# Two heads side by side in the array's rows, for the token products of a chunked attention

## Chip, cores and metric

One core of a Trainium2 chip runs one program. The metric is device time in microseconds (us), the median of the runs shown. Engines are named as the profile names them: PE (TensorE, its weight loads are PEld), DVE (VectorE), ACT (ScalarE), POOL (GpSimd), SP (SyncE, which here issues the DMAs).

## Reference

A linear attention with a state per head (4 batches, 8 heads, 768 tokens, 40 channels) is followed by a mixture of experts and a second feed-forward layer. Only the attention is touched here:

```python
for t in range(S):
    y[:, :, t] = np.einsum('bhd,bhde->bhe', rt, state)
    Sa = np.einsum('bhde,bhe->bhd', state, at)
    state_decay = state * wt[:, :, None, :] - np.einsum('bhd,bhe->bhde', Sa, bt)
    state = state_decay + np.einsum('bhd,bhe->bhde', vt, kt)
...
x = _moe_ref(x=x, **moe_kwargs)
return _moe2_ref(x=x, **moe2_kwargs)
```

## The kernel before

The program has two stages, one behind the other: the attention (`with ExitStack() as st`, L239 to L796), then the two feed-forward parts (L862 on), whose first matmul comes after the last instruction of the attention.

**Units.** The attention cuts the tokens into NJ = 6 chunks of C = 128. A unit n is one chunk of one batch, all 8 heads: 24 units, j = n // 4 the chunk, b = n % 4 the batch. Channels lie in the partitions, two heads in one tile: head a = 0 in rows 0 to 39, head a = 1 in rows 64 to 103 (HR = 104 rows in all), and four such pairs (HP = 4) one after the other in the free dimension. The inputs `em` come laid out so, with zeros in rows 40 to 63.

**What a unit does**, each a generator that yields segments (`Seg`):
- `decays` (L291): clamps the decays, two scans (L307, L313) for running products and their inverses, then `bt` (L326) and `at` (L329) as elementwise products, and two ACT passes that look for rare values.
- `lab_grams` (L336): the token products of `at` with `bt` (L352), evicted by ACT into `ld` (L359, four 32-row pieces a half) and `lab` (L360).
- `invert` (L373): the inverse of the small triangular blocks, on DVE and POOL, once for each chunk.
- `pre` (L421): `kt` (L432), the transposes `tp` (L438), the token products of `at` with `kt` (`lak`), the products with the old state (L458), a transpose of it (L467), and `z` (L474).
- `chain` (L479): four blocks of 32 tokens one after the other; PE (L498, L506, tiles of 32 by 32) and ACT (L502, L510) wait for each other in turn.
- `post` (L513): transposes of `u` (L522) and their copy `ut` (L525), the token products `mrv` (of `r` with `v`) and `mru` (of `r` with `u`), the state update (L539 to L547), and `yps` (L555, L566), evicted by DVE (L572).

**The token products** are made by `gram` (L405) for `lak`, `mrv` and `mru` and by `lab_grams` for `lab`: four sets in each unit. One head's channels stand in 40 of the 104 rows, and both heads of a pair are in the moving tile, so the stationary tile is padded: `bt`, `kt`, `ut`, `vt` have the shape [104, 4, 2, 128], where half a holds the rows of head a and zeros in all other rows. A matmul then goes over 104 rows, of which 64 at most are not zero by construction:

```python
for q in range(HP):
    nc.tensor.matmul(
        ps[:, q, :], lhsT=lhs[:, q, a, :], rhs=rhs[:, q, :],
        start=(q == 0), stop=True, skip_group_check=True,
    )
```

Half a = 0 makes four matmuls into one PSUM bank (`psg`, 3 buffers), is evicted (DVE L416, or ACT), then half a = 1 the same. A float32 matmul stands in the trace as two LDWEIGHTS and two MATMUL records, so a set of 8 matmuls has 16 of each. The padded tiles cost two elementwise operations each, one a half, of which the second may go to POOL (`spare_pool`, L626), and the zeros are written once by POOL (L730, L738).

**What sets the order.** The order of all instructions is written when the program is built. `drive` (L664) takes segments from nine flows by a model of the engines' clocks (`clk`): a segment has a PE time `pe`, an activity weight `w` for a model of TensorE's clock, the engine that evicts and its time, and what it needs. Where the model sees PE wait or its clock about to fall, `idle` (L651) puts in spare matmuls (L654). Each engine then runs its own list in that order.

**Start.** SP loads `e` for units 0 to 3 and 4 (L261), with nothing to wait for; `load_mid` brings `kr`, `v`, `bk`.

Of the kernel before, what the change touches and what calls it, by code (L numbers as in the profile page):

```python
# [18 lines left out]
C = 128  # L19
# [3 lines left out]
HALF = (slice(0, 64), slice(64, HR))  # L23
# [18 lines left out]
POOLED = 1  # L42
# [29 lines left out]
def tile_kernel(ctx, tc, em, tm, qr, qk, qv, qw, qa, qb, w_gate, w1, w2, u1, u2, u3, u_out, out):  # L72
# [8 lines left out]
    make_identity(nc, ident)  # L81
# [157 lines left out]
    with ExitStack() as st:  # L239
# [19 lines left out]
        def load_e(n, t):  # L259
            for c in (slice(0, WC), slice(WC, EC)) if not n else (slice(0, EC),):  # L260
                nc.sync.dma_start(out=t[:, c], in_=em[n // NB, n % NB, :, c])  # L261

        def load_late(n):
            d = un[n]
            d["rt"] = r_ring[n % 2]
            nc.sync.dma_start(
                out=d["rt"].rearrange("p g c -> p (g c)"), in_=em[n // NB, n % NB, :, EC + HP * C:EC + 2 * HP * C]
            )
            d["late"] = sent(0.6)

        def load_v(n):
            j, b = jb(n)
            for a in range(2):
                nc.sync.dma_start(
                    out=pads[3][64 * a:64 * a + D, :, a],
                    in_=em[j, b, 64 * a:64 * a + D, EC + 2 * HP * C:].rearrange("e (g c) -> e g c", c=C),
                )
            un[n]["vt_"] = sent(0.7)

        def load_mid(n):  # L280
            j, b = jb(n)
            d = un[n]
            nc.sync.dma_start(out=kr.rearrange("p g c -> p (g c)"), in_=em[j, b, :, EC:EC + HP * C])
# [7 lines left out]
        def decays(n, e, ready, bt):  # L291
# [6 lines left out]
            p = d["p"] = hold.tile([HR, HP, C + 1], F32, tag="p", name="p", bufs=LOOK + 2)  # L298
            ip = hold.tile([HR, HP, C + 1], F32, tag="ip", name="ip", bufs=LOOK)
            at = hold.tile([HR, HP, C], F32, tag="at", name="at", bufs=LOOK)  # L300
# [17 lines left out]
            d["bt_"] = []  # L318
# [14 lines left out]
            nc.scalar.activation(out=off, in_=ew, func=AF.Abs, bias=wmid)  # L333
            nc.scalar.activation(out=off, in_=off, func=AF.Relu, bias=wrad, accum_out=beyond[:, n:n + 1])

        def lab_grams(n):  # L336
# [6 lines left out]
            lab = None  # L343
            for a in range(2):
                s = Seg(pe=0.87, w=0.81, eng="A", cost=1.05, needs=[d["at_"], *d["bt_"]],
                        gate=lambda: count["chain"] > n - LOOK)
                yield s
                if lab is None:
                    lab = d["lab"] = hold.tile([C, H, C - 32], F32, tag="lab", name="lab", bufs=LOOK)
                ps = psg.tile([C, HP, C], F32, tag="g", name="psg")  # L350
                for q in range(HP):
                    nc.tensor.matmul(  # L352
                        ps[:, q, :], lhsT=bt[:, q, a, :], rhs=at[:, q, :],
                        start=(q == 0), stop=True, skip_group_check=True,
                    )
# [49 lines left out]
        def gram(lhs, rhs, res, tag, bufs, needs):  # L405
            for a in range(2):
                s = Seg(pe=0.87, w=0.81, eng="V", cost=0.6, needs=needs)
                yield s
                ps = psg.tile([C, HP, C], F32, tag="g", name="psg")
                for q in range(HP):  # L410
                    nc.tensor.matmul(  # L411
                        ps[:, q, :], lhsT=lhs[:, q, a, :], rhs=rhs[:, q, :],
                        start=(q == 0), stop=True, skip_group_check=True,
                    )
# [6 lines left out]
        def pre(n):  # L421
# [5 lines left out]
            kt_ = []  # L427
            for a, r in enumerate(HALF):
                key, eng = ("P", nc.gpsimd) if a and spare_pool() else ("V", nc.vector)
                kt_.append(Seg(eng=key, cost=1.3 if key == "P" else 0.6, needs=[d["mid"], d["ip_"]]))  # L430
                yield kt_[a]
                eng.tensor_tensor(out=kt[r, :, a], in0=kr[r], in1=ip[r], op=ALU.mult)  # L432
# [4 lines left out]
            for q in range(HP):  # L437
                nc.tensor.transpose(tp[:, q, 0:HR], ip[:, q, :], ident[0:HR, 0:HR])  # L438
# [18 lines left out]
            for q in range(HP if j else 0):  # L457
                nc.tensor.matmul(  # L458
                    zf[:, q, 0:HR], lhsT=at[:, q, :], rhs=s[:, q, :],
# [53 lines left out]
        def post(n):  # L513
            j, b = jb(n)
            d, u, s = un[n], u_ring[n % 2], s_t[b]
            ut_ = Seg(pe=0.44, eng="A", cost=1.0, needs=lambda: [d["u_"]], gate=lambda: count["chain"] > n)
# [7 lines left out]
            for a, r in enumerate((slice(0, 64), slice(64, HR))):  # L524
                nc.scalar.activation(out=ut[r, :, a], in_=ups[r], func=AF.Copy)  # L525
# [28 lines left out]
            for q in range(HP if j else 0):  # L554
                nc.tensor.matmul(  # L555
                    yps[:, q, :], lhsT=d["sd"][:, q, :], rhs=rt[:, q, :],
# [68 lines left out]

        def spare_pool():  # L626
            return clk["P"] + POOLED < max(clk["E"], clk["V"])

# [545 lines left out]
```

## Time and profile before

| | us |
|---|---|
| median of 3 runs | 2256.01 |
| the runs | 2254.65, 2272.37, 2256.01 |
| the profiled execution | 2262.95 |
| its span, first to last instruction | 2261.2 |
| PE busy in the span (share) | 2210.5 (98%) |
| DVE, ACT, POOL busy | 1108.2, 619.7, 324.2 |

All rows below are of the profiled execution, with time from the start of its span. A busy PE in such a table is the union of its records, which overlap; the distance from one run of records to the next tells what a run costs. The granted clock (PEclk) is 1.00 where TensorE ran at its level of 2.4 GHz and 0.50 at that of 1.2 GHz.

### The profile page before, as it was taken

Reading aid. Unit: us, or ns where it says so; the run is one execution under the profiler, and the core shown is the slowest. Engines: PE = TensorE matmul, PEld = TensorE weight load, DVE = VectorE, ACT = ScalarE, POOL = GpSimd, SP = SyncE. Lnnn points to the kernel's source line nnn. Section 1 sums busy time; section 2 is a strip of 40 time slices with the busy share of each in tenths; the row PEclk is TensorE's granted clock in tenths of the full one; section 3 lists DMA queues with packets and bytes.
Section 4 is the critical chain, followed back from the end, with each engine's and each line's share of the span. In section 5 each row is a group of like instructions: output and inputs, shape, how many; then the busy total and the mean of one; then the engine's idle time right before and its main releaser. Section 6 shows DMA issues by size and latency. Waiting matters only on the chain.

```text
span 2261.2 us, 37488 instructions
## 1 busy us (share of the span) xinstructions
PE 2210.5 (98%) x15933; PEld 1989.1 (88%) x15933; DVE 1108.2 (49%) x1896; ACT 619.7 (27%) x1239; POOL 324.2 (14%) x478
## 2 busy tenths in 40 slices
PE   5899999999999999999999999999999999999999
PEld 5888888899789999999989989999999999988888
DVE  8788667542344366556555443333343343442332
ACT  3544444322332133122122122121121121222221
POOL 6457356250000010011101000000000000000000
PEclk7899999997999999999999999999999999999999
DMA  4243333221201011111111000000000000100000
GB/s 114 71 123 96 102 83 88 66 82 36 66 27 33 1 39 44 43 36 56 36 39 44 25 26 20 8 26 14 13 26 12 15 27 7 55 6 21 15 12 24
DMA packets 71320, 94.98 MB, mean 42 GB/s; under 512 B 6981, under 2 KB 55877, under 8 KB 71149
## 3 DMA queue, kind: packets, MB, share of 16 engines
q1 hardware_dynamic: 71149, 92.56, 14.7%
q8 instruction: 125, 2.05, 0.4%
q14 instruction: 46, 0.38, 0.1%
HBM read 80.74 MB, written 11.80 MB: 41 GB/s over the span
## 4 chain that ended last, share of the span: by engine, by line
PE 74%; ACT 0%; issue 0%
PE ps L222 33%; PE ps L215 31%; PE pu L215 9%; PE gps L215 0%; PE xt L1025 0%; PE tps L909 0%; PE ct L947 0%; ACT acc L1059 0%; PE t L925 0%; PE t L919 0%
## 5 line engine op out<-in xcount | busy, mean ns | idle before, releaser
L222 PE MATMUL ps<-w2h,h 128*128 128x320 f32 x3072 | 693.0, 309 | 0.0
L222 PEld LDWEIGHTS ps<-w2h,h 128*128 128x128 f32 x3072 | 517.6, 188 | 4.5
L963 ACT ACTIVATE h<-ps 128x512 fp32r<-128x512 f32 x384 | 229.9, 599 | 999.5 <-PE ps L215 985.4
L964 DVE SCALAR_TENSOR_TENSOR h<-ps,h 128x512 fp32r<-128x512 f32 x384 | 265.7, 692 | 456.4 <-ACT h L963 455.4
L222 PE MATMUL ps<-w2l,h 128*128 128x320 f32 x1536 | 474.2, 309 | 0.0
L215 PE MATMUL ps<-xh,w1l 128*128 128x512 f32 x1152 | 330.9, 395 | 5.2 <-DVEq L856 5.2
L215 PE MATMUL ps<-xh,w1h 128*128 128x512 f32 x1152 | 327.4, 392 | 0.0
L984 DVE SCALAR_TENSOR_TENSOR acc<-ps,lg,acc 128x320 f32<-128x320 f32 x336 | 184.9, 550 | 255.2 <-PE ps L222 253.7
L222 PEld LDWEIGHTS ps<-w2l,h 128*128 128x128 f32 x1536 | 288.2, 188 | 4.0
L215 PEld LDWEIGHTS ps<-xh,w1h 128*128 128x128 f32 x1152 | 216.7, 188 | 48.6
L215 PEld LDWEIGHTS ps<-xh,w1l 128*128 128x128 f32 x1152 | 212.1, 188 | 46.5 <-issue 5.4
L215 PE MATMUL ps<-xl,w1h 128*128 128x512 f32 x768 | 239.4, 393 | 0.0
L215 PEld LDWEIGHTS ps<-xl,w1h 128*128 128x128 f32 x768 | 144.5, 188 | 34.1
L215 PE MATMUL pu<-xh,uq 128*128 128x512 f32 x648 | 171.2, 394 | 0.0
L416 DVE TENSOR_TENSOR gr<-psg,mask 128x512 f32<-128x512 f32 x144 | 97.7, 689 | 94.8 <-PE psg L411 93.8
L215 PEld LDWEIGHTS pu<-xh,uq 128*128 128x128 f32 x648 | 120.3, 188 | 25.2
L135 POOL TENSOR_TENSOR f<-f,m 128x384 f32<-128x384 f32 (+2 forms) x24 | 24.2, 1009 | 666.3 <-DVE m L133 405.7
L391 POOL TENSOR_TENSOR tmp<-lt,tt 128x87 f32<-128x87 f32 (+24 forms) x186 | 106.5, 572 | 60.3 <-DVE lt L369 46.2
L395 POOL TENSOR_TENSOR tt<-tt,tmp 128x87 f32<-128x87 f32 (+24 forms) x186 | 110.6, 595 | 14.6
L1045 DVE TENSOR_TENSOR g<-pu,g 128x512 f32<-128x512 f32 x72 | 49.8, 692 | 99.9 <-PE pu L215 99.9
L352 PE MATMUL psg<-at,bt 104*128 104x128 f32 x384 | 54.5, 300 | 29.8 <-DVE at L329 28.8
L510 ACT ACTIVATE u<-z 32x320 f32<-32x320 f32 x96 | 41.1, 429 | 138.0 <-PE z L506 137.9
(158 smaller groups left out, 2359.4 us busy)
## 6 DMA issues: line engine op xcount, KB each, us to landing
e<-in_em_dram SPq DMA_DIRECT2D x23, 626.0 KB
r<-in_moe_w_dram SPq DMA_DIRECT2D x32, 320.0 KB
r<-in_moe_w_dram SPq DMA_DIRECT2D x32, 256.0 KB
bk<-in_tm_dram SPq DMA_DIRECT2D x24, 320.0 KB
kr<-in_em_dram SPq DMA_DIRECT2D x24, 208.0 KB
r<-in_em_dram SPq DMA_DIRECT2D x24, 208.0 KB
raw<-in_moe_w_dram SPq DMA_DIRECT2D x12, 384.0 KB
r<-in_moe_w_dram SPq DMA_DIRECT2D x64, 64.0 KB
```

The costliest lines, as they stand in the source:

```text
L135: nc.gpsimd.tensor_tensor(out=f, in0=f, in1=m.bitcast(F32), op=ALU.mult)
L215: nc.tensor.matmul(ps, lhsT=a, rhs=b, start=(n == 0), stop=(n == len(seq) - 1))
L222: nc.tensor.matmul(ps, lhsT=a, rhs=b, start=(n == 0), stop=(n == last))
L352: nc.tensor.matmul(ps[:, q, :], lhsT=bt[:, q, a, :], rhs=at[:, q, :], start=(q == 0), stop=True, skip_group_check=True,)
L391: eng.tensor_tensor(out=t, in0=lt[:, m:m + 1, m + 1:32].to_broadcast([128, n, w]), in1=tt[:, 0:n, m:m + 1].to_broadcast([128, n, w]), op=A ...
L395: eng.tensor_tensor(out=tt[:, 0:n, m + 1:32], in0=tt[:, 0:n, m + 1:32], in1=t, op=ALU.subtract)
L416: nc.vector.tensor_tensor(out=t, in0=ps, in1=mask.unsqueeze(1).to_broadcast([C, HP, C]), op=ALU.mult)
L510: nc.scalar.activation(out=u[r, :, 0:D], in_=zh[r, :, 0:D], func=AF.Copy)
L963: nc.scalar.activation(out=h[:, 0], in_=ps, func=AF.Relu)
L964: nc.vector.scalar_tensor_tensor(out=h[:, 1], in0=ps, scalar=0.0, in1=h[:, 0].bitcast(F32), op0=ALU.max, op1=ALU.subtract)
L984: nc.vector.scalar_tensor_tensor(out=acc[:, i], in0=ps, scalar=pr[:, i, e:e + 1], in1=acc[:, i], op0=ALU.mult, op1=ALU.add,)
L1045: nc.vector.tensor_tensor(out=g, in0=ps, in1=g, op=ALU.max)
```

## The change

The two heads of a pair get 64 rows of the array each. `bt`, `kt`, `ut`, `vt`, and `at`, `ip`, `p`, `kr`, `rt`, `e` become tiles of 128 rows, in which rows 40 to 63 and 104 to 127 are zero (or, for the decays, without effect); the padded halves are gone. A new function `products` makes both heads' matmuls in turn, head a on array rows 64a to 64a + 63, each head into a PSUM bank of its own, and both banks are evicted after it. Its segment has pe = GRAM = 1.05 where there were two of 0.87. `psg` has 4 buffers for 3, `psy` 1 for 2. `bt` and `kt` are one DVE operation each, `ut` one ACT copy, `vt` one DMA; POOL has none of them. The zeros are written into rows 96 to 127 before the first loads, and the identity is made after them.

```diff
-POOLED = 1
+GRAM = 1.05
...
-    make_identity(nc, ident)
...
-        psg = pool(st, "psg", 3, space=PSUM)
+        psg = pool(st, "psg", 4, space=PSUM)
-        psy = pool(st, "psy", 2, space=PSUM)
+        psy = pool(st, "psy", 1, space=PSUM)
...
-            for a in range(2):
-                nc.sync.dma_start(
-                    out=pads[3][64 * a:64 * a + D, :, a],
-                    in_=em[j, b, 64 * a:64 * a + D, EC + 2 * HP * C:].rearrange("e (g c) -> e g c", c=C),
-                )
-            un[n]["vt_"] = sent(0.7)
+            nc.sync.dma_start(out=pads[3][0:HR].rearrange("p g c -> p (g c)"), in_=em[j, b, :, EC + 2 * HP * C:])
+            un[n]["vt_"] = sent(0.6)
...
-            for a, r in enumerate(HALF):
-                key, eng = ("P", nc.gpsimd) if a and (n < NB or spare_pool()) else ("V", nc.vector)
-                s = Seg(eng=key, cost=1.3 if key == "P" else 0.6, needs=[d["ip_"]])
-                d["bt_"].append(s)
-                yield s
-                eng.tensor_tensor(out=bt[r, :, a], in0=eb[r], in1=d["ip"][r], op=ALU.mult)
+            d["bt_"] = Seg(eng="V", cost=0.6, needs=[d["ip_"]])
+            yield d["bt_"]
+            nc.vector.tensor_tensor(out=bt, in0=eb, in1=d["ip"], op=ALU.mult)
...
+        def products(lhs, rhs):
+
+
+            ps = [psg.tile([C, HP, C], F32, tag="g", name="psg") for _ in range(2)]
+            for q in range(HP):
+                for a in range(2):
+                    r = slice(64 * a, 64 * a + 64)
+                    nc.tensor.matmul(
+                        ps[a][:, q, :], lhsT=lhs[r, q, :], rhs=rhs[r, q, :],
+                        start=(q == 0), stop=True, skip_group_check=True, tile_position=(64 * a, 0),
+                    )
+            return ps
...
-            for a in range(2):
-                s = Seg(pe=0.87, w=0.81, eng="A", cost=1.05, needs=[d["at_"], *d["bt_"]],
-                        gate=lambda: count["chain"] > n - LOOK)
-                yield s
...
+            s = Seg(pe=GRAM, w=0.8, eng="A", cost=2.1, needs=[d["at_"], d["bt_"]],
+                    gate=lambda: count["chain"] > n - LOOK)
+            yield s
+            lab = d["lab"] = hold.tile([C, H, C - 32], F32, tag="lab", name="lab", bufs=LOOK)
+            for a, ps in enumerate(products(bt, at)):
...
-            for a in range(2):
-                s = Seg(pe=0.87, w=0.81, eng="V", cost=0.6, needs=needs)
-                yield s
...
+            s = Seg(pe=GRAM, w=0.8, eng="V", cost=1.2, needs=needs)
+            yield s
+            for ps in products(lhs, rhs):
...
-            for a, r in enumerate((slice(0, 64), slice(64, HR))):
-                nc.scalar.activation(out=ut[r, :, a], in_=ups[r], func=AF.Copy)
+            nc.scalar.activation(out=ut[0:HR], in_=ups, func=AF.Copy)
...
-            pads = [ring.tile([HR, HP, 2, C], F32, name=x) for x in ("bt", "kt", "ut", "vt")]
+            pads = [ring.tile([128, HP, C], F32, name=x) for x in ("bt", "kt", "ut", "vt")]
...
+            low = slice(96, 128)
+            nc.vector.memset(es[0][low], 0.0)
+            for t in es[1:] + [e]:
+                nc.gpsimd.memset(t[low], 0.0)
             ready = {}
+            nc.gpsimd.memset(kr[low], 0.0)
+            make_identity(nc, ident)
...
-            for t in bts + pads[1:2]:
-                nc.gpsimd.memset(t, 0.0)
...
-                for t in u_ring + s_t + pads[2:]:
+                for t in u_ring + s_t:
                     nc.gpsimd.memset(t, 0.0)
+                for t in r_ring + pads[2:]:
+                    nc.gpsimd.memset(t[low], 0.0)
```

## Rows read from the trace of the kernel before

**Rows 1.** Windows: length; busy PE, PEld, DVE, ACT, POOL; granted clock; DMA share, GB/s.

```profile
155.70:418.00 262.30, 255.19 (x3433) 234.04 (x3433) 187.22 (x283) 118.30 (x296) 140.48 (x201) 1.00 0.36 95
...
495.30:585.30 90.00, 84.73 (x1000) 77.13 (x998) 28.34 (x45) 20.00 (x43) 2.83 (x2) 0.85 0.15 41
585.30:2261.20 1675.90, 1672.57 (x9139) 1493.97 (x9139) 733.31 (x1298) 386.55 (x659) 49.09 (x48) 1.00 0.09 27
0.00:74.60 74.60, 44.25 (x285) 42.94 (x286) 65.18 (x120) 29.96 (x83) 45.45 (x93) 0.75 0.39 96
74.60:155.70 81.10, 77.13 (x1024) 70.16 (x1022) 61.00 (x95) 41.46 (x106) 47.49 (x68) 1.00 0.39 103
```

**Rows 2.** Groups by line, 155.7 to 418.0: busy us, mean ns, idle before.

```profile
L416 DVE TENSOR_TENSOR gr<-psg,mask 128x512 f32<-128x512 f32 x74 | 50.0, 687 | 28.3 <-PE psg L411 27.6
L502 ACT ACTIVATE zs<-z 32x320 f32<-32x320 f32 x48 | 20.4, 424 | 43.4 <-PE z L498 43.3
L326 DVE TENSOR_TENSOR bt<-e,ip 64x512 f32<-64x512 f32 (+1 forms) x22 | 18.4, 838 | 0.3
L432 DVE TENSOR_TENSOR kt<-kr,ip 64x512 f32<-64x512 f32 (+1 forms) x18 | 16.8, 933 | 0.7
L329 DVE TENSOR_TENSOR at<-e,p 104x512 f32<-104x512 f32 x13 | 11.3, 867 | 0.1
```

**Rows 3.** Timeline of PE, 190 to 200: start us, us, what, records, idle before.

```profile
191.95 1.90 PE L474 MATMUL z<-v,gr 128*128 128x40 f32 x16
193.67 0.62 PE L522 MATMUL ups<-ident,u 128*104 128x128 f32 x4
194.13 1.95 PE L352 MATMUL psg<-at,bt 104*128 104x128 f32 x16
195.92 1.06 PE L411 MATMUL psg<-r,vt 104*128 104x128 f32 x8
197.22 1.16 PE L411 MATMUL psg<-r,vt 104*128 104x128 f32 x8 [0.24 <-ACT lab L360]
198.71 0.27 PE L539 MATMUL dps<-v,kb 128*40 128x40 f32 x2 [0.33 <-ACT lab L360]
```

**Rows 4.** Timeline of PE, 203 to 212.

```profile
204.36 0.76 PE L506 MATMUL z<-zs,td 32*32 32x40 f32 x16
205.04 1.07 PE L566 MATMUL yps<-gr,kb 128*40 128x128 f32 x16
206.05 0.76 PE L498 MATMUL z<-u,lab 64*32 64x40 f32 x16
```

**Rows 5.** Groups by line, 0 to 74.6: the `lab` products.

```profile
L352 PE MATMUL psg<-at,bt 104*128 104x128 f32 x96 | 18.4, 371 | 29.2 <-DVE at L329 28.8 <-ACT off L333 0.4
```

**Rows 6.** Timeline of ACT, 190 to 200: the eviction of `lab`.

```profile
195.55 1.11 ACT L359 ACTIVATE ld<-psg 32x128 f32<-32x128 f32 x4
...
198.55 0.41 ACT L502 ACTIVATE zs<-z 32x320 f32<-32x320 f32 x1
```

**Rows 7.** Timeline of all engines, 0 to 16: the start.

```profile
0.80 2.11 SPq L261 DMA_DIRECT2D e<-in_em_dram  x5
1.15 0.49 DVE L726 MEMSET ends<- 104x517 f32 x1
3.92 2.16 DVE L306 TENSOR_SCALAR e<-e 104x512 f32<-104x512 f32 x1 [2.01 <-DMA e<-in_em_dram]
9.57 0.68 DVE L329 TENSOR_TENSOR at<-e,p 104x512 f32<-104x512 f32 x1
14.40 1.70 POOL L326 TENSOR_TENSOR bt<-e,ip 40x512 f32<-40x512 f32 x1 [3.11 <-DVE ip L313]
14.96 1.68 DVE L329 TENSOR_TENSOR at<-e,p 104x512 f32<-104x512 f32 x1
```

**Rows 8.** Windows late in the attention.

```profile
510.00:530.00 20.00, 20.00 (x153) 18.07 (x154) 2.77 (x4) 4.61 (x10) 0.00 (x0) 0.53 0.04 10
550.00:560.00 10.00, 10.00 (x138) 9.29 (x135) 2.96 (x5) 2.24 (x5) 0.00 (x0) 1.00 0.15 39
```

More of the change, by code (lines that the diff above doesn't have):

```diff
@@ L22 @@
 HR = 64 + D
-HALF = (slice(0, 64), slice(64, HR))
 WC = HP * (C + 1) + 1
@@ L260, in load_e @@
             for c in (slice(0, WC), slice(WC, EC)) if not n else (slice(0, EC),):
-                nc.sync.dma_start(out=t[:, c], in_=em[n // NB, n % NB, :, c])
+                nc.sync.dma_start(out=t[0:HR, c], in_=em[n // NB, n % NB, :, c])
         def load_late(n):
@@ L266, in load_late @@
             nc.sync.dma_start(
-                out=d["rt"].rearrange("p g c -> p (g c)"), in_=em[n // NB, n % NB, :, EC + HP * C:EC + 2 * HP * C]
+                out=d["rt"][0:HR].rearrange("p g c -> p (g c)"), in_=em[n // NB, n % NB, :, EC + HP * C:EC + 2 * HP * C]
             )
@@ L282, in load_mid @@
             d = un[n]
-            nc.sync.dma_start(out=kr.rearrange("p g c -> p (g c)"), in_=em[j, b, :, EC:EC + HP * C])
+            nc.sync.dma_start(out=kr[0:HR].rearrange("p g c -> p (g c)"), in_=em[j, b, :, EC:EC + HP * C])
             d["v"] = tokp.tile([C, H, D], F32, tag="v", name="v", bufs=3)
@@ L297, in decays @@
             yield d["ip_"]
-            p = d["p"] = hold.tile([HR, HP, C + 1], F32, tag="p", name="p", bufs=LOOK + 2)
-            ip = hold.tile([HR, HP, C + 1], F32, tag="ip", name="ip", bufs=LOOK)
-            at = hold.tile([HR, HP, C], F32, tag="at", name="at", bufs=LOOK)
+            p = d["p"] = hold.tile([128, HP, C + 1], F32, tag="p", name="p", bufs=LOOK + 2)
+            ip = hold.tile([128, HP, C + 1], F32, tag="ip", name="ip", bufs=LOOK)
+            at = hold.tile([128, HP, C], F32, tag="at", name="at", bufs=LOOK)
             d["bt"] = bt
@@ L332, in decays @@
             off = chp.tile([HR, HP, C], F32, tag="off", name="off")
-            nc.scalar.activation(out=off, in_=ew, func=AF.Abs, bias=wmid)
+            nc.scalar.activation(out=off, in_=ew[0:HR], func=AF.Abs, bias=wmid)
             nc.scalar.activation(out=off, in_=off, func=AF.Relu, bias=wrad, accum_out=beyond[:, n:n + 1])
+        def products(lhs, rhs):
[8 more added lines that the diff above has]
+            return ps
         def lab_grams(n):
@@ L342, in lab_grams @@
             ld = blk[j]["ld"]
-            lab = None
-            for a in range(2):
-                s = Seg(pe=0.87, w=0.81, eng="A", cost=1.05, needs=[d["at_"], *d["bt_"]],
-                        gate=lambda: count["chain"] > n - LOOK)
-                yield s
[L348 to L355, printed above, removed]
+            s = Seg(pe=GRAM, w=0.8, eng="A", cost=2.1, needs=[d["at_"], d["bt_"]],
[3 more added lines that the diff above has]
+            for a, ps in enumerate(products(bt, at)):
                 hs = slice(HP * a, HP * a + HP)
@@ L405, in gram @@
         def gram(lhs, rhs, res, tag, bufs, needs):
-            for a in range(2):
-                s = Seg(pe=0.87, w=0.81, eng="V", cost=0.6, needs=needs)
-                yield s
[L409 to L414, printed above, removed]
+            s = Seg(pe=GRAM, w=0.8, eng="V", cost=1.2, needs=needs)
+            yield s
+            for ps in products(lhs, rhs):
                 t = gr.tile([C, HP, C], F32, tag=tag, name="gr", bufs=bufs)
@@ L426, in pre @@
             kt = pads[1]
[L427 to L432, printed above, removed]
+            kt_ = [Seg(eng="V", cost=0.6, needs=[d["mid"], d["ip_"]])]
+            yield kt_[0]
+            nc.vector.tensor_tensor(out=kt, in0=kr, in1=ip, op=ALU.mult)
             d["kb_"] = Seg(pe=0.38, w=0.81, eng="V", cost=0.8, needs=[d["mid"], d["ip_"]],
@@ L437, in pre @@
             for q in range(HP):
-                nc.tensor.transpose(tp[:, q, 0:HR], ip[:, q, :], ident[0:HR, 0:HR])
+                nc.tensor.transpose(tp[:, q, 0:HR], ip[0:HR, q, :], ident[0:HR, 0:HR])
             tpv = tp.rearrange("t g (a x) -> t g a x", x=64)[:, :, :, 0:D]
@@ L458, in pre @@
                 nc.tensor.matmul(
-                    zf[:, q, 0:HR], lhsT=at[:, q, :], rhs=s[:, q, :],
+                    zf[:, q, 0:HR], lhsT=at[0:HR, q, :], rhs=s[:, q, :],
                     start=(q == 0), stop=True, skip_group_check=True,
@@ L515, in post @@
             d, u, s = un[n], u_ring[n % 2], s_t[b]
-            ut_ = Seg(pe=0.44, eng="A", cost=1.0, needs=lambda: [d["u_"]], gate=lambda: count["chain"] > n)
+            ut_ = Seg(pe=0.44, eng="A", cost=0.6, needs=lambda: [d["u_"]], gate=lambda: count["chain"] > n)
             yield ut_
@@ L555, in post @@
                 nc.tensor.matmul(
-                    yps[:, q, :], lhsT=d["sd"][:, q, :], rhs=rt[:, q, :],
+                    yps[:, q, :], lhsT=d["sd"][:, q, :], rhs=rt[0:HR, q, :],
                     start=(q == 0), stop=True, skip_group_check=True,
```

15 lines of the change are left out of this document (6 added, 9 removed).

## The prediction

> **What bounds the kernel now.** I read the windows by stage first, then the groups by line of the stage with most units, then PE's timeline inside it. The feed-forward stage (585.3 to 2261.2) keeps PE at 1672.57 of 1675.90 us and is not touched [rows 1]; it starts when the attention is over, so what the attention saves comes off the end one for one. The attention has three parts. Up to 74.6 DVE is busy 65.18 of 74.60 us and PE 44.25: DVE bounds it. From 74.6 on PE is busy all the time (77.13 of 81.10, 255.19 of 262.30, 84.73 of 90.00), while DVE has 187.22 and ACT 118.30 of 262.30 us [rows 1]. In that stretch ACT ran 48 of the four-per-unit `zs` copies [rows 2]: 12 units, 21.86 us each, of which DVE needs 15.6 and ACT 9.9. So PE sets the period, and time taken from PE is worth itself until something else is late.
>
> **What a set of token products costs.** `lab`'s 16 records start at 194.13, the next run at 195.92: 1.79 us, 0.112 for each record [rows 3]. Four sets are 7.16 of the 21.86 us. What the new form costs is not in the trace; I bound it. `z` also loads 128 columns of weights, moves only 40 columns, and takes 1.72 us for 16 (191.95 to 193.67) [rows 3]: at this shape the weight load sets the pace, not the columns that move. So the upper end is that the two heads' loads take turns: 16 times 0.112, 1.79, plus 0.1 for a change of array shape (below), 1.89. The lower end is that each pair runs fully beside each other: 8 times 0.112, 0.90. The nearest row is L566. Its matmuls alternate between columns 0 to 39 and 64 to 103 of the array, with 128 moving columns, and 16 records take 1.01 us (205.04 to 206.05) [rows 4]: eight pairs, not sixteen turns. It differs in that its loads are 40 columns wide and the two tiles lie in columns. I take its pace with the wider load: 1.03 us. The difference to now is 0.76 us.
>
> The Trainium skill, page "TensorE: Matmul & The Clock Gate", section "LDWEIGHTS (loading the stationary operand)", says that a load's time goes by its columns and not by its rows, so that 64 rows would load no faster than 104; by this alone a set stays at 1.79 and nothing is gained. The same page, "Part 3: Packing small matmuls — row/col tiling", says that loads and matmuls on different row groups overlap; by this a set is near 0.9. No row of this trace has two row groups in turn; the first reading is the first rival below.
>
> A change of shape costs too: a 32 by 32 run of 16 records is 0.68 us from its start to the next (204.36 to 205.04) [rows 4], where one full-array run follows the other without a gap, 16 times 0.112 being the whole 1.79 [rows 3]. L566's 1.01 has its own exit in it, 8 times 0.11 being 0.88. Full-array work ahead of a set will pay some 0.1 where it paid nothing. I put this at half of the sets, 0.05 each (between 0 and 0.1). Net: 0.71 us a set.
>
> **How many sets count.** 96 sets; 96 records of `lab`, 6 sets, stand before 74.6, mostly beside DVE's work [rows 5]. The other 90 are in the PE-bound part: 90 times 0.71 is 63.9 us.
>
> **What does not shrink with them.** After `lab` PE already waits for ACT: `mrv` and `dps` start late at 197.22 and 198.71, so that 16 records take 2.79 us, 1.0 too long [rows 3], because `psg` is held until ACT has read `lab`, from 195.55 until its next copy at 198.55 [rows 6]. ACT's 3.0 us stay. Four buffers instead of three, of which a set takes two at once, leave the distance from `lab` to the first reuse of its banks as it was. `lab` and `mrv` together get 1.5 us shorter while this eviction starts little earlier: one of `ut`'s two copies goes ahead of it, but the chain's next copy (198.55) [rows 6] waits behind it in ACT's queue as before. I charge 0.5 us for each of the 18 later `lab` sets (0 to 1.5): 9 us. Elsewhere the two evictions of a set follow the whole set instead of the first lying beside the second half: a set of 1.03 and two evictions of 0.69 [rows 2] make 2.4 us to the second result, 1.79 and one make 2.5, so who waits for it sees no change. That leaves 54.9 us.
>
> **DVE, POOL, memory.** `bt` and `kt` were 18.4 and 16.8 us of DVE in 12 units, besides POOL's halves. As one operation of 128 rows each costs what `at` does, 0.87 [rows 2]; 64 and 104 rows cost the same in this table, so rows do not count. DVE falls by about (35.2 - 24 times 0.87) / 12, 1.2 us a unit, hidden under PE: worth nothing directly, and cover for the evictions. The same holds for `psy` with one buffer (one `yt` a unit, long read before the next unit's `yps`), for `vt` as one DMA, for the wider scans, and for the removed POOL zeros. If that cover went, `psy` would cost one 0.7 us eviction a unit, 16 us in all.
>
> **The start.** New: SP's first DMA waits until DVE has cleared 32 rows of 1541 columns. The 517-column memset took 0.49 us [rows 7], so this is 1.5, and `e` is issued at some 2.6 instead of 0.80; the first clamp moves from 3.92 by 1.8 us [rows 7]. Behind it on SP the loads of units 1 to 3, `kr`, `v`, `bk` and `e` of unit 4 wait in turn for four POOL memsets (1.5 each) and `kr`'s 0.5, done by 7 us, before DVE wants them. Against this `at`, which took 1.68 us where POOL worked on `bt` beside it and 0.68 where not [rows 7], gets 1.0 us shorter three times. Net -1.2 (from -3 to +2).
>
> **Sum.** 54.9 + 1.2 is 56.1 off the profiled execution's 2262.95 (span 2261.2 and 1.75 around it): 2206.9. The median of the runs is 6.94 lower than that execution: **2200 us**.
>
> **Rivals.**
> 1. *The two row halves take turns.* For it: `z`, where the load alone sets the pace [rows 3]. Against: L566's pairs [rows 4]. A set stays 1.79 plus 0.05: 90 times 0.05 more, 1.2 less, so 2262.95 + 3.3 - 6.94 = 2259: no change.
> 2. *Another engine becomes the bound.* With 18.8 us a unit, DVE's 14.4 is 77%, and ACT's eviction of `lab`, the chain's turns with ACT and DVE's long scans fall together more often, so that PE's waits grow. If half of 63.9 is lost so, and 1.2 stays: 2262.95 - 33.2 - 6.94 = 2223.
> 3. *TensorE's clock falls; slower.* Between 510 and 530 the granted clock is 0.53, and PE issues 153 MATMUL records where 550 to 560 at 1.00 has 138 in 10 us: 20 us for 11 us of work, so a stretch costs some 10 [rows 8]. It came in the last units, whose `lab` sets the order makes some units ahead, so that the chain with its 32 by 32 tiles and `z` were most of PE's work. The change takes just the dense full-width work out of every unit, and the order holds against it only by a model. From six new stretches on it eats the gain; with eight, one in three units, 2200 + 80 = 2280. With one to three: 2210 to 2230. Against it: from 74.6 to 418 the granted clock is 1.00 in both stages [rows 1], and a set of two heads still fills 128 rows, only for a shorter time. The one stretch there may also go: 2190.
>
> **How the numbers follow.** Main case 0.58, with its own range of 2178 to 2218. Rival 2: 0.17. Rival 3: 0.11 with one to three stretches, 0.06 with eight or more. Rival 1: 0.08. The low end, 2168, is the main case with the sets at 0.9 (90 times 0.13, 12 us), no charge after `lab` (9) and the cold stretch gone (10), not all at once; the high end, 2242, takes in rival 2 with some more and the light form of rival 3, and leaves out rival 1 and the heavy clock, with the edges 0.2. One per cent of 2256, about what a measurement of this kernel can tell from no change, is 22.6: faster is below 2233.4, slower above 2278.6. Faster: 0.58 + 0.16 + 0.10 = 0.84. Same: the rest of 2 and 3 and rival 1, 0.11. Slower: 0.05.
>
> **What would show it.** In the new profile a set of 16 records should take 1.0 to 1.1 us from its start to the next run, in 64-row shapes; 1.8 is rival 1. Units of the middle stage should be 18.5 to 19.5 us apart, with PE still nearly always busy and DVE at 75 to 80%; 20 and more with PE idle and waits for L416 or L360 is rival 2. The granted clock should stay 1.00 up to the late units. The first clamp should start near 5.7, the first chain near 73. The feed-forward stage should last 1676 us as now; if it doesn't, the ground of this sum is wrong.

## The result, and the profile after

The kernel after takes 2270.99 us (median of 20 runs, 2260.37 to 2292.33), the kernel before beside it 2258.68 (20 runs, 2251.07 to 2272.37): a ratio of 1.0056 [1.0034 to 1.0079]. Forecast were 2200, with a range of 2168 to 2242. So the change costs half a per cent where it was to bring two and a half. The profiled execution took 2267.62 (span 2265.9; before 2262.95 and 2261.2).

The windows of after, cut at the same events as [rows 1] (first chain, the start of the middle units, their end, first matmul of the feed-forward part); columns as there:

```profile
0.00:64.80 64.80, 36.81 (x295) 34.62 (x296) 54.36 (x111) 24.78 (x69) 35.75 (x88) 0.82 0.46 112
64.80:161.50 96.70, 91.61 (x1116) 80.00 (x1117) 62.52 (x104) 44.64 (x119) 41.14 (x64) 0.77 0.34 90
161.50:436.30 274.80, 263.19 (x3436) 232.39 (x3432) 163.53 (x263) 108.87 (x282) 124.33 (x192) 0.84 0.35 92
436.30:589.20 152.90, 148.13 (x2088) 131.33 (x2087) 58.85 (x101) 38.01 (x90) 35.21 (x64) 0.91 0.21 59
589.20:2265.90 1676.70, 1673.39 (x9139) 1494.67 (x9139) 732.88 (x1298) 386.26 (x659) 48.94 (x48) 1.00 0.09 27
```

The feed-forward stage is as long as it was (1676.7 for 1675.9). The first chain starts 9.8 us earlier (64.8 for 74.6), and yet the feed-forward part starts 3.8 later (589.2 for 585.4). The last but two column tells why: TensorE was granted 0.77, 0.84 and 0.91 in the three parts of the attention, where [rows 1] has 1.00, 1.00 and 0.85. PE's busy share says nothing of it: 502.94 of 524.40 us, 96%, where before had 97%.

The sets themselves became what was forecast. PE's timeline of after, between 199 and 202:

```profile
199.69 0.76 PE L484 MATMUL z<-u,lab 64*32 64x40 f32 x16
200.38 1.16 PE L333 MATMUL psg<-at,kt 64*128 64x128 f32 x16
201.47 0.76 PE L492 MATMUL z<-zs,td 32*32 32x40 f32 x16
```

From 200.38 to 201.47 are 1.09 us for 16 records, where [rows 3] had 1.79. The 64-row shape stands in the operands (64*128). DVE's part is lighter as well; groups by line of after, 161.5 to 436.3, beside [rows 2]:

```profile
L405 DVE TENSOR_TENSOR gr<-psg,mask 128x512 f32<-128x512 f32 x72 | 46.3, 685 | 43.7 <-PE psg L333 43.3
L418 DVE TENSOR_TENSOR kt<-kr,ip 128x512 f32<-128x512 f32 x13 | 11.5, 884 | 1.0 <-DMA kr<-in_em_dram 0.6
L316 DVE TENSOR_TENSOR bt<-e,ip 128x512 f32<-128x512 f32 x12 | 8.6, 715 | 15.3 <-PE psg L333 15.2
```

`bt` and `kt` are 8.6 and 11.5 us where the padded halves took 18.4 and 16.8, and DVE waits for PE's products 43.3 us ahead of L405 (27.6 before): DVE has become less of a limit, not more.

**The sum of it.** I add up the stretches at 1.2 GHz (granted clock 0.50) between the first chain and the feed-forward part, without the fall in the last microseconds ahead of that part, which both kernels have (2.7 us before, 0.9 after): 23.9 us in one stretch before, 160.4 us in 13 stretches after. A chain step takes 1.20 there for 0.69, a set 2.01 for 1.09, so between 0.43 and, at most, 0.50 of such time is lost: of the 136.5 us more, 59 to 68. The attention from the first chain on grew by 13.6 (510.8 to 524.4). At full clock it would have shrunk by 45 to 55, where 54.9 had been forecast. Below, "at full clock" is the attention less half of its time at 1.2 GHz: 498.9 before, 444.2 after. So counted, -9.8 (start), -54.7 (attention at full clock), +68.2 (clock) and +0.9 (feed-forward) are 4.6 of the span's 4.7. That they add up shows nothing of the two large terms, since one is defined by the other and the half is the upper end.

The single runs show them without a profile. In the 20 runs of after the granted clock of a run lies between 0.946 and 0.961, which is 176 to 247 us at 1.2 GHz in its span (twice the missing share of it), and the span grows by 0.44 us with each us of it (correlation 0.97): the lower end, 59 us, is the nearer one. Carried on to no time at 1.2 GHz at all, which is an extrapolation, this line ends at 2181 us, and the line through 40 runs of the kernel before, made beside the experiments, at 2235. They are some 55 us apart (standard error 5), the start included. So the saving is there, and the slow clock takes it back.

By kind of record (from each to the next, slow time taken back by the 0.46 of a set): sets 190 us to 114, spare matmuls 5 to 23, chain 118 and 118, all else 188 to 197. By its clock model the order puts in more spares than it did, and they do not hold the clock. The spare matmuls of the whole program in after, 159 in 318 records (before had 92 spares in all, 17 of them after the first chain; after has 69 there):

```profile
L636 PE MATMUL spare<-ones x318: 274/275/583, 1.1 to 579.8; 128*128 128x128 f32 x159
```

**Where the clock falls.** Two kinds of places stand ahead of the 13 falls. Seven (85 of the 160 us) come with no wait of PE above 0.7 us, behind one recurring part of a unit. PE's timeline of after, ahead of the fall at 267.5:

```profile
260.91 0.57 PE L424 MATMUL tp<-ident,ip 104*128 104x104 f32 x4
261.42 1.16 PE L333 MATMUL psg<-at,kt 64*128 64x128 f32 x16
262.51 0.76 PE L492 MATMUL z<-zs,td 32*32 32x40 f32 x16
263.19 1.14 PE L444 MATMUL z<-s,at 104*128 104x104 f32 x8
264.26 0.76 PE L484 MATMUL z<-u,lab 32*32 32x40 f32 x16
264.95 0.57 PE L453 MATMUL sps<-ident,s 104*104 104x104 f32 x4
265.35 1.00 PE L460 MATMUL z<-v,gr 128*128 128x40 f32 x8
266.29 0.76 PE L492 MATMUL z<-zs,td 32*32 32x40 f32 x16
266.97 1.49 PE L460 MATMUL z<-v,gr 128*128 128x40 f32 x8
...
268.39 1.27 PE L484 MATMUL z<-u,lab 64*32 64x40 f32 x16
```

PE never pauses here, but it goes from tiles of 32 by 32 to products that move only 40 columns, and the one set of token products among them is 1.09 us long. Before, that set was 1.79 us long. The one fall of before, at 511.0 in the late units [rows 8], has the same part ahead of it, and there with a whole set of 104-row records, cut in two by a chain step; PE's timeline of before has its second half and the end of the part:

```profile
504.34 1.16 PE L411 MATMUL psg<-at,kt 104*128 104x128 f32 x8
505.43 0.76 PE L506 MATMUL z<-zs,td 32*32 32x40 f32 x16
...
509.89 1.09 PE L474 MATMUL z<-v,gr 128*128 128x40 f32 x8
```

So the length of that one set does not decide alone. Three more falls (58 us) come behind a wait of PE above 1 us, once for DVE's `kt` (2.15) and twice for its eviction of a product, `gr` (1.86 and 1.13); the last three (17 us) lie in the first units. The clearest of those behind a wait, windows of after around it:

```profile
141.20:168.50 27.30, 23.89 (x388) 20.99 (x389) 22.51 (x37) 11.43 (x28) 5.44 (x12) 1.00 0.48 124
168.50:189.00 20.50, 20.50 (x168) 18.46 (x168) 7.37 (x12) 5.36 (x12) 0.00 (x0) 0.50 0.29 94
189.00:212.90 23.90, 21.79 (x337) 19.00 (x336) 16.44 (x25) 13.41 (x34) 13.65 (x22) 1.00 0.35 93
```

20.5 us at 1.2 GHz hold 168 MATMUL records with PE busy throughout; the 23.9 behind it hold 337. What PE waited for ahead of it, in its timeline and in DVE's:

```profile
165.47 0.73 PE L492 MATMUL z<-zs,td 32*32 32x40 f32 x16 [0.27 <-DVE td L364]
168.35 1.98 PE L333 MATMUL psg<-at,kt 64*128 64x128 f32 x16 [2.15 <-DVE kt L418]
```

```profile
163.20 2.12 DVE L364 STREAM_TRANSPOSE td<-tt 128x1024 f32<-128x1024 f32 x1
165.17 1.37 DVE L557 TENSOR_TENSOR yt<-yps,p 40x512 f32<-40x512 f32 x2
166.56 1.64 DVE L418 TENSOR_TENSOR kt<-kr,ip 128x512 f32<-128x512 f32 x1
```

`kt` stood behind a 2.1 us transpose and `yt`, and PE had no set left to lie over them. The wait itself is 2.15 us; the clock that falls behind it loses some 9 or 10 more.

### The profile page after: what moved, and what is told of

The parts are those of the page before. It is cut to its first block, busy times and chain, and to the rows that moved or that the text cites. A ratio compares the mean times of both kernels' runs of the same rounds, so it can differ in the third digit from the quotient of the medians.

```text
span 2265.9 us, 37515 instructions
## 1 busy us (share of the span) xinstructions
PE 2213.1 (98%) x16067; PEld 1973.0 (87%) x16067; DVE 1072.1 (47%) x1874; ACT 602.6 (27%) x1215; POOL 285.4 (13%) x455
## 4 chain that ended last, share of the span: by engine, by line
PE 74%; ACT 0%; issue 0%
PE ps L220 33%; PE ps L213 31%; PE pu L213 9%; PE gps L213 0%; PE xt L1013 0%; PE tps L897 0%; PE ct L935 0%; ACT acc L1047 0%; PE t L913 0%; PE t L907 0%
## 5 line engine op out<-in xcount | busy, mean ns | idle before, releaser
L405 DVE TENSOR_TENSOR gr<-psg,mask 128x512 f32<-128x512 f32 x144 | 92.5, 685 | 117.9 <-PE psg L333 117.0
L390 POOL TENSOR_TENSOR tt<-tt,tmp 128x87 f32<-128x87 f32 (+24 forms) x186 | 105.7, 568 | 14.6
L492 PE MATMUL z<-zs,td 32*32 32x40 f32 x1536 | 82.2, 211 | 1.2 <-ACT zs L488 1.0
```

What stands on the lines that cost most here:

```text
L390: eng.tensor_tensor(out=tt[:, 0:n, m + 1:32], in0=tt[:, 0:n, m + 1:32], in1=t, op=ALU.subtract)
L405: nc.vector.tensor_tensor(out=t, in0=ps, in1=mask.unsqueeze(1).to_broadcast([C, HP, C]), op=ALU.mult)
L492: nc.tensor.matmul(zh[r, h, 0:D], lhsT=td[r, 8 * b + hx(h), :], rhs=zs[r, h, :], start=(h == 0), stop=True, skip_group_check=True, tile_po ...
```

## Experiments

Each ratio is to runs of the kernel before made beside it, whose medians were 2262.14 us (e1 to e4), 2262.54 (e5 to e8) and 2262.06 (e9 to e12). The table gives what the profiled execution of each kernel shows between first chain and feed-forward part.

| | time, us | ratio [95%] | first chain | attention | at 1.2 GHz (stretches) | at full clock |
|---|---|---|---|---|---|---|
| before | 2258.68 | 1 | 74.6 | 510.8 | 23.9 (1) | 498.9 |
| after | 2270.99 | 1.0056 [1.0034, 1.0079] | 64.8 | 524.4 | 160.4 (13) | 444.2 |
| e1_half_sets | 2339.83 | 1.0329 [1.0279, 1.0378] | 73.1 | 602.2 | 382.3 (14) | 411 |
| e2_no_pool_halves | 2270.06 | 1.0036 [1.0008, 1.0064] | 76.6 | 519.6 | 34.1 (2) | 502.5 |
| e3_spare_per_step | 2281.26 | 1.0080 [1.0051, 1.0110] | 65.2 | 538.4 | 88.7 (5) | 494 |
| e4_plan_durations | 2234.05 | 0.9886 [0.9836, 0.9935] | 75.1 | 475.0 | 84.7 (6) | 432.6 |
| e5_heads_in_turn | 2364.29 | one run | 68.7 | 618.6 | 310.9 (8) | 463 |
| e6_start_order | 2282.82 | 1.0082 [1.0053, 1.0112] | 70.1 | 543.7 | 92.8 (4) | 497.3 |
| e7_plan_and_start | 2228.07 | 0.9862 [0.9799, 0.9925] | 68.5 | 472.4 | 65.3 (6) | 439.7 |
| e8_plan_dve_act | 2231.39 | 0.9859 [0.9811, 0.9907] | 73.4 | 479.7 | 78.5 (8) | 440.5 |
| e9_before_replanned | 2316.38 | 1.0235 [1.0175, 1.0295] | 79.2 | 567.1 | 149.9 (5) | 492 |
| e10_after_again | 2285.06 | 1.0088 [1.0058, 1.0117] | 66.6 | 551.3 | 220.8 (15) | 440.9 |
| e11_hot55 | 2236.66 | 0.9878 [0.9844, 0.9913] | 66.7 | 501.5 | 134.2 (4) | 434.4 |
| e12_spares_by_mean | 2288.30 | 1.0135 [1.0071, 1.0200] | 68.6 | 534.1 | 147.3 (5) | 460 |

The last column sorts the kernels by their sets: with full sets (before, e2, e6, e9) it is 492 to 503, with paired heads and at most 71 spares (after, e10, e4, e7, e8, e11) 433 to 444. That gap is the gain of the change, and it is there in each of the six; e12 and e3, with 101 and 199 spares, lie at 460 and 494. The column beside it is what differs most from kernel to kernel.

**Is it the lost dense work, or the 64-row shape?** The first kernel is before, in its own order, with full-array sets cut to half their records:

```diff
-                ps = psg.tile([C, HP, C], F32, tag="g", name="psg")
-                for q in range(HP):
+                if not a:
+                    ps = psg.tile([C, HP, C], F32, tag="g", name="psg")
+                for q in range(0 if a else HP):
```

> The kernel before, its order of PE instructions kept, but the second head's matmuls of every token-product set are left out (its eviction reads the first head's bank again), so the output lacks them. A set is then 8 full-array records of 0.9 us instead of 16: the same PE time goes as in the change, with no 64-row shape, no more spare matmuls, the old start. Theory A (the clock falls because dense work has gone out of every unit): after 75 us at least 120 us lie at the 1.2 GHz level, against 31 before and 160 after the change, and the time is 2235 to 2275. Theory B (matmuls on half the rows, two at a time, count less for the clock than full-array ones): below 60 us at 1.2 GHz and 2180 to 2205.

It came out at 2339.83, above all that was expected, with 382.3 us at 1.2 GHz. Its timeline at full clock, and its window from first chain to feed-forward part:

```profile
153.13 1.16 PE L413 MATMUL psg<-r,ut 104*128 104x128 f32 x8
154.22 0.76 PE L500 MATMUL z<-u,lab 32*32 32x40 f32 x16
```

```profile
73.10:675.30 602.20, 564.04 (x5800) 510.41 (x5798) 304.47 (x480) 202.87 (x498) 225.98 (x337) 0.68 0.26 69
```

A set takes 1.09 us (153.13 to 154.22), as the paired one does, but over the full array. The clock falls the more for it (0.68), and its order has only 17 spares there. So the clock also falls for less dense work without any 64-row shape. Each of its 14 falls comes less than 5 us behind a wait of PE of 0.5 to 1.7 us, or within one. Most of these waits are for the chain's copies on ACT (20.7 us in all ahead of L508), where before has no wait: the dense work had covered them. So e1 does not part the thinner work from the waits that it uncovers. The falls of after without a wait are the evidence for the first.

**Do the two row halves really run beside each other?** After, with the loops over heads and pairs exchanged, so that no two neighbours lie in different halves:

```diff
-            for q in range(HP):
-                for a in range(2):
+            for a in range(2):
+                for q in range(HP):
```

> The changed kernel, with the four matmuls of head 0 ahead of the four of head 1 in every set, so that two matmuls in turn use the same 64 rows; same instructions otherwise. If the sets' 1.09 us come from two heads on different rows side by side, a set now takes 1.75 to 1.9 us at 2.4 GHz and, at half the rows, keeps the clock worse: over 200 us at 1.2 GHz after the first chain, 2330 us or more. Rival (a load of 64 rows is shorter by itself): sets stay at 1.1 us and the time at 2271.

A set takes 1.64 us at full clock in its timeline (3.02 at 1.2 GHz):

```profile
179.03 1.71 PE L333 MATMUL psg<-at,kt 64*128 64x128 f32 x16
180.67 0.76 PE L492 MATMUL z<-zs,td 32*32 32x40 f32 x16
```

The same matmuls in another sequence are 0.55 us longer, so in after the pairs do overlap. The Trainium skill, page "TensorE: Matmul & The Clock Gate", "Part 3: Packing small matmuls — row/col tiling", says so; 1.09 against 1.64 agrees. The 1.64 lies under the 1.75 to 1.9 expected. The single records of this set tell why: within one head the MATMULs start 0.112 us apart, as they do with 104 rows [rows 3], but the last four of head 0 run beside the first three of head 1. The same page of the Trainium skill says that rows do not count in a weight load ("LDWEIGHTS (loading the stationary operand)"); 0.112 us a record with 64 rows as with 104 agrees.

This run also shows something that was not asked of it; its window from first chain to feed-forward part:

```profile
68.70:687.30 618.60, 610.79 (x6635) 548.67 (x6635) 285.79 (x463) 191.51 (x487) 197.28 (x318) 0.75 0.26 70
```

PE is busy 610.79 of 618.60 us and the sets are nearly as long as before's, but with one head's 64 rows at a time the clock is 0.75, with 310.9 us at 1.2 GHz. Seven of its eight falls come without a wait above 0.5 us. So long sets did not hold the clock here as before's 104-row sets did: e1 shows that a fall does not need the 64-row shape, not that the shape is without effect. It is one run.

**Chance or order?** After once more, unchanged:

> The changed kernel once more, unchanged, on the chip of the other three: 2262 to 2280, with 12 to 15 stretches at 1.2 GHz after the first chain and 130 to 180 us in them, if the falls are the order's and not one execution's chance; below 80 us if they are chance.

The loss came again (ratio 1.0088), more of it than expected: 2285.06 us for at most 2280, and 220.8 us in 15 stretches for at most 180. Eleven of after's 13 falls come again within 33 PE records of the same place, of 16067 in all. Nine of them are at 174.8, 215.8, 253.3, 270.4, 338.7, 359.1, 386.4, 451.3 and 526.4 us, where after has 168.5, 212.9, 250.4, 267.5, 339.2, 363.1, 390.4, 448.4 and 523.5; four falls of e10 have none beside them in after. How long one lasts differs (71.7 us from 526.4 here, 17.1 from 523.5 there). So where the clock falls belongs for the most part to the order, and for how long differs from run to run.

**Where did the 9.8 us at the start come from?** My first idea was POOL: in before it makes the second halves of `bt` and `kt` in the start. The second kernel is before with these on DVE:

```diff
-                key, eng = ("P", nc.gpsimd) if a and (n < NB or spare_pool()) else ("V", nc.vector)
+                key, eng = ("V", nc.vector)
...
-            key, eng = ("P", nc.gpsimd) if a and spare_pool() else ("V", nc.vector)
+            key, eng = ("V", nc.vector)
```

> The kernel before, with every second half of bt and kt on DVE instead of POOL; nothing else. Theory A (the earlier start of the first chain, 64.8 for 74.6 us, came from kt's POOL half, which stood behind the inversion): the first chain starts before 69 us, and the time falls by 3 to 8 us, to 2250 to 2256. Rival (the start came earlier because the sets are shorter on the slow clock): the first chain stays at 73 to 76, the time within 3 us of before or higher by DVE's added work.

The first chain came at 76.6, later than in before: that theory fell. Another idea was the order of the first units; before with a smaller EARLY:

```diff
-EARLY = 6
+EARLY = 4
```

> The kernel before, with one number of its order changed (EARLY 4 for 6), so that the first unit's kt stands on DVE's list ahead of the inversion's last transpose, as it does in the changed kernel; sets, tiles and POOL halves as before. Theory (the changed kernel's earlier first chain, 64.8 for 74.6 us, is the order alone): the first chain starts at 63 to 68 us, and the time is 4 to 10 us below before, 2248 to 2256. Rival (it needs the shorter sets): 70 us or later, no change of the time.

The chain began at 70.1, 4.5 us earlier and not the 63 to 68 expected, and the time grew. The window from 43.4 shows a reason:

```profile
43.40:94.60 51.20, 35.35 (x222) 33.30 (x223) 34.51 (x71) 12.43 (x34) 18.77 (x45) 0.50 0.15 41
```

TensorE stays at 1.2 GHz from 43.4 to 94.6, where before has 27.3 us from the same time on, and two of the four stretches behind the first chain follow pauses of PE above 1 us. A few instructions moved in before's order also bring the clock down.

**Can the clock be held?** First with a spare matmul behind each step of the chain:

```diff
+                    idle(1)
...
+                idle(1)
```

> The changed kernel with one spare full-array matmul after each of the seven PE steps of every chain: 289 spares where the change has 159, 130 times 0.22 us, 29 us more work for PE. Theory A (the clock): the time at 1.2 GHz after 75 us falls from 160 to below 80 us, worth 40 us or more, and the time is 2245 to 2262 in spite of the added work. Rival (the sum fails because another engine or the chain's turns bound the stage): PE's added work lies in waits or adds to the end, no gain: 2270 to 2300.

The time at 1.2 GHz went from 160.4 to 88.7, not quite to the 80 expected, but the time to 2281.26, as the rival had it. Its timeline shows the price of one spare:

```profile
206.20 0.49 PE L638 MATMUL spare<-ones 128*128 128x128 f32 x2
206.62 1.51 PE L553 MATMUL yps<-gr,kb 128*40 128x128 f32 x24
...
208.75 0.49 PE L638 MATMUL spare<-ones 128*128 128x128 f32 x2
209.07 0.52 PE L424 MATMUL tp<-ident,ip 104*128 104x104 f32 x4
```

Between two other shapes one costs 0.32 to 0.42 us from its start to the next run, not the 0.22 of its two records. The 130 spares after the first chain that after does not have are some 47 us at 0.36 each; the 71.7 us less at 1.2 GHz give back 33 (at 0.46). The difference, 14, is what the attention grew by (524.4 to 538.4).

Next I gave the planner the durations that the trace shows. It had put a chain step at 0.23 us where 0.69 is measured, so its model of the clock saw the thin work too short. After, with all PE times of the plan so mended (some of the lines):

```diff
-GRAM = 1.05
+GRAM = 1.09
...
-                    s = Seg(pe=0.23, w=0.3, eng="A", cost=0.32, needs=[s])
+                    s = Seg(pe=0.68, w=0.2 * i, eng="A", cost=0.42, needs=[s])
...
-                s = Seg(pe=0.24 if i else 0.62, w=0.25, eng="A", cost=0.32, needs=[s])
+                s = Seg(pe=0.68, w=0.2, eng="A", cost=0.42, needs=[s])
...
-                d["s_"] = Seg(pe=0.9, w=0.78, eng="V", cost=1.2)
+                d["s_"] = Seg(pe=1.25, w=0.85, eng="V", cost=1.3)
```

> The changed kernel, with the planner's PE times and weights set to what the profile after shows (a set 1.09, a chain step 0.68 where the plan had 0.23 and 0.24, the rest by 10 to 40%). 132 spares against 159, another order. Theory A (the plan's model of the clock was on a wrong time scale and so didn't see the low stretches): less than 100 us at 1.2 GHz after 75 us, 2225 to 2250. Rival (the model's scale does not matter, low density is in the work itself): 130 us or more, 2262 to 2280.

2234.05, faster than both kernels, with 84.7 us at 1.2 GHz. Units are 18.3 us apart in its undisturbed stretches. One late fall, in PE's timeline, follows a wait of 1.74 us inside `lab`'s set:

```profile
313.48 0.49 PE L333 MATMUL psg<-at,bt 64*128 64x128 f32 x2
315.71 1.13 PE L333 MATMUL psg<-at,bt 64*128 64x128 f32 x14 [1.74 <-DVE kb L428]
```

The first chain had moved back to 75.1, so the next kernel has the smaller EARLY as well:

```diff
-EARLY = 6
+EARLY = 4
```

> The changed kernel with the plan's PE durations as in e4_plan_durations and with EARLY 4. 144 spares. If e4's start at 75 us was only its order: first chain at 61 to 66 us and 2218 to 2232 us, 5 to 12 below e4. Rival (an earlier start runs into PE's slow clock and is given back): 2230 to 2245.

2228.07, ratio 0.9862 [0.9799, 0.9925]: the lowest median of all, though e4 and e8 are level with it within the noise. The first chain, at 68.5, came later than the 61 to 66 expected. Its windows, from the first chain to the feed-forward part, of two undisturbed stretches and of a slow one:

```profile
68.50:540.90 472.40, 454.26 (x6578) 403.07 (x6576) 284.42 (x461) 191.97 (x491) 198.30 (x318) 0.93 0.33 90
```

```profile
200.00:236.00 36.00, 35.67 (x561) 31.95 (x558) 24.28 (x40) 17.36 (x46) 24.83 (x38) 1.00 0.40 107
236.00:253.00 17.00, 16.62 (x184) 14.17 (x182) 8.69 (x17) 3.68 (x8) 0.00 (x0) 0.61 0.37 95
...
380.00:536.00 156.00, 155.18 (x2407) 138.86 (x2408) 77.20 (x132) 51.47 (x124) 45.76 (x82) 1.00 0.25 71
```

From 380 to 536 the clock does not fall once, with PE at 155.18 of 156.00. The median distance of the middle units is 18.3 us (before 21.85, after 23.2). Is the gain the better plan alone? Before with the same kind of durations (some of the lines):

```diff
-                    s = Seg(pe=0.23, w=0.3, eng="A", cost=0.32, needs=[s])
+                    s = Seg(pe=0.68, w=0.2 * i, eng="A", cost=0.42, needs=[s])
...
-                s = Seg(pe=0.87, w=0.81, eng="V", cost=0.6, needs=needs)
+                s = Seg(pe=0.9, w=0.77, eng="V", cost=0.6, needs=needs)
```

> The kernel before, full-array sets, with the plan's PE durations set to what the traces show, as e4_plan_durations does for the changed kernel (a half set 0.9, a chain step 0.68). If e4's gain is the shorter sets, now kept by the clock, this kernel stays at 2245 to 2270, with PE bound by sets of 1.79. Rival (the gain of e4 is the better plan and would come without the change): 2225 to 2240.

It got slower, 2316.38, with 149.9 us at 1.2 GHz, against both expectations:

```profile
79.20:646.30 567.10, 545.90 (x6496) 501.67 (x6496) 306.96 (x469) 200.21 (x488) 234.09 (x341) 0.87 0.27 73
```

All five of its falls behind the first chain follow pauses of PE above 1 us. So the mended plan alone does not make the gain: three orders made with mended durations for the paired sets (e4, e7, e8) each came out below 2235, and the one for the full sets above 2300. It is a single order, and e6 shows that one number of the order moves this kernel by 0.8%, so a better order for the full sets is not ruled out.

Three further tries to hold the rest. DVE's and ACT's durations in the plan mended too, on top of e4 (some of the lines):

```diff
-            s = Seg(pe=GRAM, w=0.8, eng="A", cost=2.1, needs=[d["at_"], d["bt_"]],
+            s = Seg(pe=GRAM, w=0.8, eng="A", cost=3.1, needs=[d["at_"], d["bt_"]],
...
-            s = Seg(pe=GRAM, w=0.8, eng="V", cost=1.2, needs=needs)
+            s = Seg(pe=GRAM, w=0.8, eng="V", cost=1.35, needs=needs)
```

> The changed kernel with the plan's PE durations as in e4_plan_durations and also those of DVE and ACT (a decay 3.2 for 2.2, a transpose 2.1 for 1.2, a lab eviction 3.1 for 2.1, the rest by some 10%); 186 spares. In e4 the late stretches at 1.2 GHz follow waits of PE for DVE, once for a chunk. Theory (the clock falls where the order makes PE wait, because the plan doesn't see it): below 60 us at 1.2 GHz after the first chain, and 2215 to 2235. Rival (the stretches come from low density in the chain itself): 85 us or more, 2235 to 2260 with the added spares.

2231.39, as fast as e4; the time at 1.2 GHz, 78.5, missed the expectation of under 60. On top of e7 a higher level below which the plan puts spares in:

```diff
-HOT = 0.42
+HOT = 0.55
```

> e7_plan_and_start with the plan's own bound for spare matmuls raised (HOT 0.55 for 0.42): 157 spares for 144, at other places. Theory (each stretch at 1.2 GHz costs half its length, and the plan can keep some away): 30 to 60 us at 1.2 GHz after the first chain, 2208 to 2228. Rival (added spares cost as much as they keep): 2228 to 2245.

2236.66, in the rival's range, with 134.2 us at 1.2 GHz in the profile instead of 30 to 60; one slow stretch of 85.3 us began at 40.5, ahead of the first chain. The profiled execution, 2246.09, is one of the slower ones. And, on e7, spares by the model's mean:

```diff
+            if clk["h"] < 0.55 and s.w < 0.5:
+                return True
```

> e7_plan_and_start with spare matmuls put ahead of every chain step or z product at which the plan's running mean of activity is low: 197 spares for 144, 53 times 0.22 to 0.36 us, 12 to 19 us of PE. Theory A: below 35 us at 1.2 GHz after the first chain, worth 15 us or more of the 33 that e7 still loses, so 2215 to 2232. Rival: 60 us or more at 1.2 GHz, 2235 to 2255.

2288.30, above what the theory and its rival had: more spares (101 after the first chain for 48) and 147.3 us at 1.2 GHz, where under 35 were expected. Three of its five falls follow pauses of PE of 2.3 to 3.3 us within `psg<-r,ut`: the order with the new spares has waits that e7's, of 1.6 us at most there, has not. Why one order waits there and another doesn't was not taken further.

## Why the prediction failed, point by point

- **What bounds the kernel** stood. What the attention gains or loses reaches the end one for one, and the feed-forward part lasts 1676.7.
- **A set of token products** stood: 1.09 us for 1.03 plus 0.05. Rival 1, the row halves in turn, did not happen; e5 shows what it would have been, 1.64 and not 1.79.
- **The charge after `lab`**, 9 us on top of the waits of before, did not come. PE waited for `lab`'s eviction 9.3 us in all before and 9.9 after. Where nothing lies between, `lab` and the next set took 4.58 us before (194.13 to 198.71 [rows 3]) and take 2.85 after (232.31 to 235.16): 1.73 less, for the 0.92 that two sets at 0.71 less the charge give. Where another run lies between, as at 410.19, the pair is 1.6 over two free sets, as the charge had it, but over all units the waits did not grow by it.
- **The sum of the sets**, 54.9, came out as 45 to 55 at full clock, but not by its own terms, and so in part by luck. The sets alone gave 76: 0.86 each, of which 0.70 is the shorter set and the rest shorter waits, for 0.61 with the charge. The spares that the plan put in took 18 back and all else 9, which the sum had left out.
- **Rival 2, another engine**: DVE got shorter (163.53 of 274.80, 13.6 us a unit for the 14.4 forecast), and e7's units come 18.3 us apart, under the 18.8 of that rival. As a bound it did not happen. As a trigger it did: waits of 1.1 to 2.2 us for DVE preceded three of the falls.
- **The start** was mis-sized. The first clamp came at 5.93 for the 5.7 forecast, but the first chain at 64.8 for 73:

```profile
2.82 2.34 SPq L259 DMA_DIRECT2D e<-in_em_dram  x5
...
5.93 0.95 DVE L300 TENSOR_SCALAR e<-e 128x512 f32<-128x512 f32 x1 [2.18 <-DMA e<-in_em_dram]
...
58.32 0.68 DVE L418 TENSOR_TENSOR kt<-kr,ip 128x512 f32<-128x512 f32 x1
...
62.44 2.07 DVE L364 STREAM_TRANSPOSE td<-tt 128x1024 f32<-128x1024 f32 x1
```

  In this timeline of the start `kt` stands ahead of the 2.1 us transpose that the first chain needs; in before it stood behind it, at 65.66. The plan had reordered the start. The order alone gave 4.5 us (e6), POOL's halves nothing (e2); the rest was not isolated.
- **Rival 3, the clock: here the prediction failed.** The step is the premise of the main case that the granted clock would stay 1.00 up to the late units, with its argument that "a set of two heads still fills 128 rows, only for a shorter time". The mechanism was named, with its place and nearly its size: from six stretches on, each costing 10 us, it was to eat the gain. There were 13, of 12 us on average and so costing some 5 each, a loss of 59 to 68. The weight was wrong, 0.06 for the heavy form. The clock of 1.00 in [rows 1] showed that before's mix held it, and said nothing of a mix with 0.7 us less dense work a set; the one row that bore on that, the fall in [rows 8] in units whose `lab` sets had run out, was read as an exception. e1 shows the fall without the change's shape, together with waits; seven falls of after show it without waits; e10 shows that it is no chance.
- **The order's clock model** was named as the guard, and its durations were not held against the trace: 0.23 us for a step that takes 0.69. [rows 4] has such a run at 0.68, so the model's fault stood in the rows before.

What stays open: e7's profiled execution, 2219.30 us, still has 65.3 us at 1.2 GHz after the first chain. Without them it would be some 30 us faster (0.46 of them), near 2190, and no run got there. What of the falls is due to thinner work and what to the waits was not parted any further.

## What to carry to other kernels

Where TensorE is busy all the time at full clock, a change that shortens its dense work must be priced twice: once for the time saved, once for what the clock does when the remaining work is thinner. Look in the profile before for a place where the dense work has already run out, and let the granted clock there bear on the forecast, not the clock of the stages that are full alone. Where a planner writes the order, hold its durations against the trace before its guard is trusted, and mend them with the change: here that turned +0.6% into -1.1% (e4), and into -1.4% with a smaller EARLY (e7).

## What the runs showed of the hardware that was not expected

- The clock falls with PE busy without a gap: 260.9 to 267.5 in after has no pause, only 32 by 32 tiles, 40-column products and short sets.
- Sets of nearly the old length with one head's 64 rows at a time did not hold the clock: 0.75 in e5, with PE busy 99% of the time.
- Two row halves side by side each keep the pace of one: 0.112 us a record with 64 rows as with 104, so a set is 1.09 us in alternation and 1.64 with one head behind the other.
- A wait costs several times its length when the clock falls behind it: 20.5 us at 1.2 GHz, some 9 or 10 lost, after 2.15.
- A slow stretch lasts for different times at the same place, 17.1 or 71.7 us within seven PE records in after and e10; the longest, in e5, was 126.3 us from 41.6 on.
- One spare matmul between two other shapes takes 0.32 to 0.42 us, for 0.22 of its own records in a row of full-array work.
